# A change of order and of sums in a fused attention and dense-layer kernel on one core

## The chip, the cores and the metric

The kernel runs on one core of a Trainium2 chip. The metric is the device time of one execution in microseconds. "Before" is the kernel that is changed, "after" is the changed one. TensorE multiplies matrices, ScalarE computes tanh and exp, VectorE and GpSimd do elementwise work, and the sync engine issues most of the DMAs; the trace calls it SPq.

## The reference, cut to what matters

```python
def _attn_ref(q, k, v, cap):                      # (8, 12, 448, 64), f32
    scores = np.matmul(q, k.transpose(0, 1, 3, 2)) / np.sqrt(64)
    scores = cap * np.tanh(scores / cap)          # cap = 30
    attn = np.exp(scores - np.max(scores, axis=-1, keepdims=True))
    attn = attn / (np.sum(attn, axis=-1, keepdims=True) + 1e-09)
    return np.matmul(attn, v)

x = attn_out.transpose(0, 2, 1, 3).reshape(3584, 768)
g = np.maximum(x @ w1, x @ w2)                    # 768 -> 1024
out = g @ w_out                                   # 1024 -> 768
```

## The kernel before

Heads are taken in pairs, 48 in all. Three pairs are a *group*, whose k, q and v are loaded, cast and transposed together, so there are 16 groups. Two pairs are a *quad*, so there are 24 quads. Iteration `t` of the main loop computes the scores of quad `t + 1`, and the product with v and the sums of exponentials of quad `t`. A token row has 448 = 3 x 128 + 64 keys; the last 64 are the *left tokens*.

The normalization goes a long way round. VectorE copies the sums, one DMA brings them into shape (`sums`), VectorE inverts them, a DMA writes 7 KB of reciprocals to DRAM (`rec_d`), two DMAs read them back spread over 128 partitions (`rec_b`, here called the broadcast), and GpSimd multiplies (`xT`). GpSimd also casts k, q and v. From group 4 on, a DMA transpose makes `qkT` of the casts. Each engine works through its own list in order, and so does the sync engine: an issue that waits holds up all issues behind it.

```python
def add(t, ab, step):                    # sums of exponentials on VectorE
    if t < NS or t >= NQ:                # NS = 5: quads 0 to 4 sum on TensorE alone
        return
    ...
    if step == 0:
        nc.vector.tensor_add(d, e_of(t, ab, 1 if ab else 0), e_of(t, ab, 2 if ab else 1))
    else:
        nc.vector.tensor_add(d, d, e_of(t, ab, 0 if ab else 2))

def pv(t, ab):
    ...                                  # product with v
    if ab:
        for m in range(2):               # left tokens: two 128*64 matmuls
            nc.tensor.matmul(ss[64 * m : 64 * m + 64, :S], ones2, expo[t, 2][:, m, :], start=True, stop=False)
        nj = NJ if t < NS else 1
        for j in range(nj):
            for m in range(4):
                x = e_of(t, m // 2, j)[:, m % 2, :] if t < NS else esum[t][:, m, :]
                nc.tensor.matmul(ss[32 * m : 32 * m + 32, :S], ones, x, start=False, stop=(j == nj - 1))
    if ab == 0:
        U[t] = upool.tile([P, 2, S], f32, name="u", bufs=3)
    ...                                  # copy to U; copy sums, DMA them into sums[t]

def invert(t):
    r = xpool.tile([32, 56], f32, name="rec_s")
    nc.vector.reciprocal(r, sums[t])
    recd[t] = dram.tile([32, 56], f32, name="rec_d")
    nc.sync.dma_start(out=recd[t], in_=r)

def spread(t):
    ...
    for h in range(2):                   # waits until rec_d has landed
        nc.sync.dma_start(out=rec[t][64 * h : 64 * h + 64, :, :], in_=lines[h : h + 1, :, :].to_broadcast([64, 2, S]))

for g in range(2, NL):                   # what an iteration loads and casts
    if g < NT:
        ...
    else:
        e = 3 * g - g % 2
        at(e - 8, load, g, "k")
        at(e - 8 + g % 2, load, g, "q")  # odd groups: q half an iteration after k
        at(e - 6, cast, nc.gpsimd, g, "k")
        at(e - 6, cast, nc.gpsimd, g, "q")
        at(e - 4, cross, g)              # the DMA transpose
        ...

for t in range(NQ):                      # main loop, cut to the order of things
    ...
    if t > 4:
        spread(t - 2)
    extra(i)                             # loads, casts, transposes of this half
    ...
    pv(t, 0)
    ...
    if t > 4:
        normalize(t - 2, 0)              # multiplies, behind the casts
        normalize(t - 2, 1)
    ...
    if t > 4:
        invert(t - 1)
    extra(i + 1)
    ...
    pv(t, 1)
    ...
```

## Time and profile before

| | before |
|---|---|
| median of 4 runs | 378.8 us (375.2 to 382.1) |
| span of the profiled run (one of 380.9 us, not of the four), granted TensorE clock | 379.2 us, 0.980 |
| fourth exp of quad 2, 7, 8, 23 ends | 44.7, 114.7, 126.5, 319.5 us |
| dense matmuls alone at the end | 59.7 us |

The windows and waits that carry the bound are in the prediction.

Columns are the start and duration in us, engine, line, operation and tiles. This is the kernel before, around 114.7 us, when iteration 7 begins:

```profile
107.62 0.33 SPq L365 DMA_DIRECT2D rec_d<-rec_s  x1
107.99 0.43 SPq L137 DMA_DIRECT2D qr<-in_q_dram  x1
...
111.07 0.60 SPq L357 DMA_DIRECT2D sums<-st  x1
111.78 1.21 SPq L435 DMA_DIRECT2D out_dram<-osb  x2
113.09 1.83 SPq L371 DMA_DIRECT2D rec_b<-rec_d  x2
115.02 4.41 SPq L268 DMA_TRANSPOSE qkT<-kqf  x1
```

The reciprocals are written at 107.62; a q load, the sums and two stores are issued before the broadcast at 113.09, which by then need not wait; the transpose starts at 115.02, 0.3 us into iteration 7. The issue of this transpose occupies the sync engine for 4.41 us.

### The profile page before, as it was taken

The page shows a single profiled execution, that of the slowest core. Times are in us where ns is not written, and L with a number is a line of the kernel's source. Part 1 is how long each engine was busy: PE and PEld are TensorE (multiplying, and loading weights), DVE is VectorE, ACT ScalarE, POOL GpSimd, SP SyncE. Part 2 cuts the span into 40 slices and gives each one's busy share as a digit, 9 for nine tenths or more (in the row PEclk, how much of TensorE's full clock was granted, in tenths as well). Part 3 has the DMA queues.
Part 4 walks back from the last instruction along what each step waited for, and adds up shares of the span by engine and source line. Part 5 has one row for each costly group of instructions (what it writes and reads, how often), then busy time and mean ns, then how long its engine had stood idle before and what let it go on. Part 6 is the DMA issues. An engine that isn't in the chain of part 4 may idle for free.

```text
span 379.2 us, 6549 instructions
## 1 busy us (share of the span) xinstructions
PE 349.0 (92%) x2492; PEld 168.2 (44%) x2492; DVE 200.6 (53%) x348; ACT 281.8 (74%) x265; POOL 150.1 (40%) x188
## 2 busy tenths in 40 slices
PE   3677986898999999999999999999989999999996
PEld 2223443443444444444444454434434444555563
DVE  4223473567665676455745654557448556633421
ACT  4999986697999989998898899889958897000000
POOL 3734135637554445444562456243644302420000
PEclk9997898999999999999999999999989999999999
DMA  7999999996788987999698959896988132422022
GB/s 251 263 209 220 274 284 223 227 193 139 215 212 221 213 232 203 223 234 255 177 213 208 251 163 250 232 242 165 216 217 213 51 91 105 122 80 95 2 83 84
DMA packets 104464, 71.56 MB, mean 189 GB/s; under 512 B 58224, under 2 KB 99440, under 8 KB 104432
## 3 DMA queue, kind: packets, MB, share of 16 engines
q1 hardware_dynamic: 102480, 67.99, 71.1%
q0 software_dynamic: 1952, 3.15, 4.5%
q8 instruction: 19, 0.31, 0.4%
q14 instruction: 13, 0.11, 0.1%
HBM read 53.48 MB, written 11.18 MB: 171 GB/s over the span
## 4 chain that ended last, share of the span: by engine, by line
PE 65%; DMA 19%; DVE 5%; SPq 4%; ACT 3%; issue 2%; POOL 1%; POOLq 0%; DVEq 0%; ACTq 0%
PE mm L396 17%; PE mm L411 16%; PE mm L408 12%; PE pv L334 6%; DMA qkT<-kqf 6%; PE s L295 6%; DMA qr<-in_q_dram 6%; DMA vr<-in_v_dram 4%; DMA rec_b<-rec_d 3%; PE pv L348 3%; PE ss L347 2%; PE s L290 1%; DVE u L351 1%; ACT expo L303 1%; ACT tanh L296 1%
## 5 line engine op out<-in xcount | busy, mean ns | idle before, releaser
L296 ACT ACTIVATE tanh<-s 128x896 bf16<-128x896 f32 x144 | 124.3, 915 | 32.5 <-PE s L295 31.1
L303 ACT ACTIVATE expo<-tanh 128x1792 bf16<-128x1792 bf16 (+1 forms) x96 | 144.9, 1510 | 0.1
L383 POOL TENSOR_TENSOR xT<-u,rec_b 128x448 bf16<-128x448 f32 x48 | 58.4, 1238 | 101.1 <-DMA rec_b<-rec_d 81.2
L411 PE MATMUL mm<-wo_sb,gT 128*128 128x384 bf16 x448 | 86.8, 330 | 0.0
L396 PE MATMUL mm<-xT,wd_sb 128*128 128x448 bf16 x384 | 79.1, 354 | 2.7 <-POOL xT L383 1.3
L351 DVE COPY u<-pv 128x448 f32<-128x448 f32 x48 | 29.9, 624 | 91.0 <-PE pv L348 78.3
L408 PE MATMUL mm<-wm_sb,xT 128*128 128x384 bf16 x336 | 66.6, 326 | 0.2 <-DVE gT L400 0.2
L411 PEld LDWEIGHTS <-gT 128*128 128x128 bf16 x448 | 43.6, 99 | 31.1 <-issue 3.6
L415 DVE COPY osb<-mm 128x384 f32<-128x384 f32 x56 | 31.1, 555 | 46.3 <-PE mm L411 46.0
L396 PEld LDWEIGHTS <-wd_sb 128*128 128x128 bf16 x384 | 37.2, 98 | 38.4 <-issue 5.9
L295 PE MATMUL s<-qkT 64*128 64x448 bf16 x288 | 43.2, 371 | 11.1 <-ACT tanh L298 3.4
L400 DVE TENSOR_SCALAR gT<-mm 128x448 bf16<-128x448 f32 x64 | 39.1, 616 | 16.8 <-PE mm L396 16.6
L408 PEld LDWEIGHTS <-xT 128*128 128x128 bf16 x336 | 32.5, 98 | 23.3 <-issue 1.9
L334 PE MATMUL pv<-expo,vp 128*64 128x448 bf16 x288 | 37.5, 370 | 0.0
L158 POOL CAST vp<-vr 128x1152 bf16<-128x1152 f32 x15 | 18.0, 1201 | 46.8 <-DMA vr<-in_v_dram 43.5
L321 DVE TENSOR_TENSOR esum<-esum,expo 128x896 bf16<-128x896 bf16 x38 | 29.9, 787 | 1.5
L319 DVE TENSOR_TENSOR esum<-expo 128x896 bf16<-128x896 bf16 x38 | 26.6, 699 | 0.0
L295 PEld LDWEIGHTS <-qkT 64*128 64x128 bf16 x288 | 9.4, 95 | 36.8 <-issue 28.7
L298 ACT ACTIVATE tanh<-s 128x896 bf16<-128x896 f32 x24 | 22.0, 917 | 4.4 <-PE s L290 3.9
L334 PEld LDWEIGHTS <-vp 128*64 128x64 bf16 x288 | 12.4, 110 | 21.3 <-issue 15.2
L232 PE MATMUL mm<-wo_sb,w2T 128*128 128x384 bf16 x96 | 19.1, 334 | 1.4 <-DVE qkT L264 1.4
L178 POOL CAST kqf<-qr 128x1152 bf16<-128x1152 f32 x12 | 14.5, 1207 | 9.6 <-DMA qr<-in_q_dram 9.4
(56 smaller groups left out, 227.7 us busy)
## 6 DMA issues: line engine op xcount, KB each, us to landing
rec_b<-rec_d SPq DMA_DIRECT2D x48, 224.0 KB
kr<-in_k_dram SPq DMA_DIRECT2D x12, 576.0 KB
qr<-in_q_dram SPq DMA_DIRECT2D x12, 576.0 KB
vr<-in_v_dram SPq DMA_DIRECT2D x12, 576.0 KB
out_dram<-osb SPq DMA_DIRECT2D x17, 384.0 KB
out_dram<-osb SPq DMA_DIRECT2D x22, 192.0 KB
osb<-in_moe_w_dram SPq DMA_DIRECT2D x6, 512.0 KB
vr<-in_v_dram SPq DMA_DIRECT2D x8, 288.0 KB
```

What stands on the lines that cost most here:

```text
L295: nc.tensor.matmul(s[:, h, :S], k0[r, j * P : (j + 1) * P], qTn[r, :])
L296: nc.scalar.activation(tanh[t, p][:, 2 * m : 2 * m + 2, :], s[:, :, :S], AF.Tanh, scale=scale / cap)
L303: nc.scalar.activation(expo[t, p], tanh[t, p][:, 0:n, :], AF.Exp, scale=float(cap))
L321: nc.vector.tensor_add(d, d, e_of(t, ab, 0 if ab else 2))
L334: nc.tensor.matmul(ps[r, :S], vp[g % 2][:, 2 * n + h, j, :], e_of(t, ab, j)[:, h, :], start=(j == 0), stop=False)
L351: nc.vector.tensor_copy(U[t][:, ab, :], ps[:, :S])
L383: eng.tensor_mul(xT[b // 2][:, hp, cs], U[t][:, ab, :], rec[t][:, ab, :])
L396: nc.tensor.matmul(ps[:, :S], wd_sb[:, c, f * P : (f + 1) * P], x[:, c, cs], start=(c == 0), stop=(c == KC - 1))
L400: nc.vector.tensor_relu(g[:, f, cs], ps[:, :S])
L408: nc.tensor.matmul(ps[:, : DM // 2], x[:, c, ts], wm_sb[:, c, hs], start=(c == 0), stop=False)
L411: nc.tensor.matmul(ps[:, : DM // 2], g[:, f, ts], wo_sb[:, f, hs], start=False, stop=(f == FC - 1))
L415: nc.vector.tensor_copy(osb[:, hs], ps[:, : DM // 2])
```

## The change

The intent was to take away the waits of the early quads and some of TensorE's work. Early v rows are loaded in one piece of 1792 bytes and cut up by the casts; `u` gets a fourth buffer; early loads are placed one by one; q of every group is loaded with its k; the broadcast is issued half an iteration sooner; multiplies stand ahead of casts; the exp of the left tokens is added on VectorE instead of by two matmuls; only quads 0 and 1 still sum on TensorE alone. The diff, cut to its core:

```diff
-        if step == 0:
+        if step == 2:                          # left tokens
+            r = slice(64 * ab, 64 * ab + 64)
+            d = esum[t][r, ab::2, :]
+            nc.vector.tensor_add(d, d, expo[t, 2][r, :, :])
+        elif step == 0:
...
-            for m in range(2):
+            for m in range(2 if t < NS else 0):
...
-            U[t] = upool.tile([P, 2, S], f32, name="u", bufs=3)
+            U[t] = upool.tile([P, 2, S], f32, name="u", bufs=4)
...
-    NS = 5
+    NS = 2
...
-            at(e - 8 + g % 2, load, g, "q")
+        at(e - 8, load, g, "q")
...                                             # early loads in a table of their own
-        if t > 4:
-            spread(t - 2)
+        if t > 3:
+            normalize(t - 2, 0)
+            normalize(t - 2, 1)
         extra(i)
...
         pv(t, 0)
-        F(8 + more8)
+        F(4)
+        add(t, 1, 0)
+        F(3 + 2 * more8)
...
-        if t > 4:
-            normalize(t - 2, 0)
-            normalize(t - 2, 1)
...
+        add(t, 0, 2)
         F(2 + more8 if more else 0)
-        add(t, 1, 0)
-        F(4 if more else 2)
+        add(t, 1, 2)
+        F(4 + more8 if more else 2)
         add(t, 1, 1)
...
+        if t > 2:
+            spread(t - 1)
         pv(t, 1)
```

More of the change, by code (lines that the diff above doesn't have):

```diff
@@ L118, in load @@
         t, m, l = raw_of(g, what)
-        if g < NT and what == "v":
-            x = rows(src, b, h0, h1).rearrange("(h r) c -> r h c", r=64)
-            for a in range(2):
-                nc.sync.dma_start(
-                    out=m[64 * a : 64 * a + 64, 2 * n0 : 2 * n1, :], in_=x[:, :, NJ * D * a : NJ * D * (a + 1)]
-                )
-            for par in range(2):
-                nc.sync.dma_start(
-                    out=l[64 * par : 64 * par + 64, n0:n1, :], in_=x[:, par::2, 2 * NJ * D :]
-                )
-            return
         if g < NT:
@@ L156, in cast @@
         x, m, l = raw_of(g, what)
+        if what == "v" and g < NT:
+            x = x[:, : L * S].rearrange("p (n c) -> p n c", c=S)
+            for h in range(2):
+                r = slice(64 * h, 64 * h + 64)
+                for a in range(2):
+                    eng.tensor_copy(
+                        vp[g % 2][64 * a : 64 * a + 64, h::2, :, :].rearrange("p n j d -> p n (j d)"),
+                        x[r, :, NJ * D * a : NJ * D * (a + 1)],
+                    )
+                eng.tensor_copy(vl[g % 2][r, :, r], x[r, :, 2 * NJ * D :])
+            return
         if what == "v":
@@ L346, in pv @@
                     x = e_of(t, m // 2, j)[:, m % 2, :] if t < NS else esum[t][:, m, :]
-                    nc.tensor.matmul(ss[32 * m : 32 * m + 32, :S], ones, x, start=False, stop=(j == nj - 1))
+                    nc.tensor.matmul(ss[32 * m : 32 * m + 32, :S], ones, x, start=(t >= NS), stop=(j == nj - 1))
         nc.tensor.matmul(ps[:, :S], vl[g % 2][:, n, :], expo[t, 2][:, ab, :], start=False, stop=True)
         if ab == 0:
-            U[t] = upool.tile([P, 2, S], f32, name="u", bufs=3)
+            U[t] = upool.tile([P, 2, S], f32, name="u", bufs=4)
         nc.vector.tensor_copy(U[t][:, ab, :], ps[:, :S])
@@ L453, in at @@
         todo[i].append((f, a))
-    for g in range(2, NL):
-        if g < NT:
-            e = 0 if g == 2 else 1
-            at(3 * g - 6 + e, load, g, "k")
-            at(3 * g - 6 + e, load, g, "q")
-            at(3 * g - 4 + e, load, g, "v")
-            at(3 * g - 4, cast, nc.gpsimd, g, "k")
-            at(3 * g - 4, cast, nc.gpsimd, g, "q")
-            at(3 * g - 2, cast, nc.gpsimd, g, "v")
-        else:
-            e = 3 * g - g % 2
-            at(e - 8, load, g, "k")
-            at(e - 8 + g % 2, load, g, "q")
-            at(e - 6, cast, nc.gpsimd, g, "k")
-            at(e - 6, cast, nc.gpsimd, g, "q")
-            at(e - 4, cross, g)
-            at(e - 4, load, g, "v")
-            at(e - 2, cast, nc.gpsimd, g, "v")
-    at(1, load, 1, "v")
-    at(2, cast, nc.gpsimd, 1, "v")
-    for c, i in enumerate((3, 3, 4, 5, 6, 7)):
-        todo[i].insert(c if i == 3 else 0, (load_w1, (c,)))
-    MS = 3
+    for g in range(NT, NL):
+        e = 3 * g - g % 2
+        at(e - 4, cross, g)
+        at(e - 8, load, g, "k")
+        at(e - 8, load, g, "q")
+        at(e - 4, load, g, "v")
+        at(e - 6, cast, nc.gpsimd, g, "k")
+        at(e - 6, cast, nc.gpsimd, g, "q")
+        at(e - 2, cast, nc.gpsimd, g, "v")
+    early = {
+        1: [(load, (1, "v"))],
+        2: [(load, (3, "k")), (load, (3, "q")), (load_w1, (0,))],
+        3: [(load_w1, (1,)), (load_w1, (2,)), (load, (2, "v"))],
+        4: [(load_w1, (3,))],
+        5: [(load_w1, (4,)), (load, (3, "v"))],
+        6: [(load_w1, (5,))],
+    }
+    for i, what in ((2, "2k"), (2, "2q"), (2, "1v"), (4, "2v"), (5, "3k"), (5, "3q"), (6, "3v")):
+        early[i].append((cast, (nc.gpsimd, int(what[0]), what[1])))
+    for i, x in early.items():
+        todo[i] += x
+    MS = 2
     fill_const(nc.vector, 0)
@@ L486 @@
     load(0, "v")
+    load(2, "k")
+    load(2, "q")
     cast(nc.vector, 0, "k", 0, 1)
@@ L489 @@
     fill_const(nc.gpsimd, 1)
+    load_w2(0)
+    load_w2(1)
     transposes(0)
@@ L502 @@
     transposes(2)
-    cast(nc.vector, 0, "v")
     cast(nc.gpsimd, 1, "k")
@@ L507 @@
         load_wo(f)
-    for c in range(3):
-        load_w2(c)
-    for c in range(3, KC):
+    for c in range(2, KC):
         load_w2(c)
@@ L527 @@
         weights(i)
-        if t % 3 == 2 and t > 2:
+        if t % 3 == 2 and t > 5:
             fill_q.append(moe(t // 3 - 1))
@@ L537 @@
             transposes(i + 3)
-        F(5 + more8 if more else 0)
-        if t > 4:
-            spread(t - 2)
+        if t == 0:
+            cast(nc.vector, 0, "v")
+        F(4 + more8 if more else 0)
+        if t > 3:
+            normalize(t - 2, 0)
+            normalize(t - 2, 1)
         extra(i)
-        F(6 if more else 3)
+        F(5 + 2 * more8 if more else 3)
         if more:
@@ L546 @@
         pv(t, 0)
-        F(8 + more8)
+        F(4)
+        add(t, 1, 0)
+        F(3 + 2 * more8)
         F(3 if more else 0)
-        if MS < i <= MS + KC:
-            subtract(i - MS - 1)
-        if t > 4:
-            normalize(t - 2, 0)
-            normalize(t - 2, 1)
+        if 3 <= i < 3 + KC:
+            subtract(i - 3)
         if more:
@@ L557 @@
         weights(i + 1)
+        if t == 4:
+            fill_q.append(moe(0))
         if i + 4 < NT * L:
             transposes(i + 4)
+        add(t, 0, 2)
         F(2 + more8 if more else 0)
-        add(t, 1, 0)
-        F(4 if more else 2)
+        add(t, 1, 2)
+        F(4 + more8 if more else 2)
         add(t, 1, 1)
         F(2 if more else 0)
-        if t > 4:
+        if 1 < t < 4:
+            spread(t - 2)
+        if t > 2:
             invert(t - 1)
-        elif t > 1:
-            spread(t - 2)
         extra(i + 1)
-        F(3 + more8 if more else 0)
+        F(2 + more8 if more else 0)
         if more:
@@ L573 @@
             ex(t + 1, 2)
+        if t > 2:
+            spread(t - 1)
         pv(t, 1)
@@ L578 @@
         F(3 if more else 0)
-        if 0 < t < 5:
+        if 0 < t < 3:
             invert(t - 1)
-        if 1 < t < 5:
+        if 1 < t < 4:
             normalize(t - 2, 0)
             normalize(t - 2, 1)
-        if MS < i + 1 <= MS + KC:
-            subtract(i - MS)
-    F(6)
-    spread(NQ - 2)
-    F(10)
+        if 3 <= i + 1 < 3 + KC:
+            subtract(i - 2)
+    F(16)
     invert(NQ - 1)
```

## The prediction

> **What bounds the kernel now.** The 48 pairs of heads run as 24 quads of two. A quad needs four rounds of tanh and exp on ScalarE; between them TensorE does scores, the product with v, sums of the exponentials, and "fills", matmuls of the dense layer put into gaps. I first read the whole page (TensorE 92%, ScalarE 74%, VectorE 53%), then the timeline of ScalarE for the end of each quad's fourth exp (21.1, 44.7, 88.1, 102.9, 126.5 us after quads 0, 2, 5, 6, 8; the last exp at 319.5), and asked for the windows between these times:
>
> ```profile
> core 0: us, PE busy (x) PEld busy (x) DVE busy (x) ACT busy (x) POOL busy (x), PEclk, DMA share, GB/s
> 21.10:44.70 23.60, 18.48 (x213) 8.04 (x209) 7.82 (x13) 23.37 (x22) 7.71 (x12) 0.86 1.07 224
> 44.70:88.10 43.40, 35.88 (x358) 18.07 (x357) 25.57 (x39) 35.02 (x33) 20.14 (x24) 0.96 0.94 225
> 88.10:102.90 14.80, 14.09 (x88) 5.93 (x87) 10.35 (x18) 11.73 (x12) 8.40 (x13) 1.00 0.90 226
> 102.90:126.50 23.60, 23.60 (x161) 11.20 (x161) 12.87 (x23) 23.36 (x22) 12.06 (x14) 1.00 0.79 201
> 126.50:319.50 193.00, 189.52 (x1219) 88.18 (x1219) 113.70 (x193) 173.64 (x164) 83.94 (x97) 0.99 0.80 198
> 319.50:379.20 59.70, 55.96 (x333) 31.42 (x329) 22.77 (x40) 0.00 (x0) 6.68 (x6) 0.99 0.26 84
> ```
>
> Read the quads per window. Two quads in 23.60 us with ScalarE 99% busy: 11.8 us is the floor of a quad. The next three took 43.4 us instead of 35.4, the one after 14.8 instead of 11.8: 11.0 us lost while ScalarE waited. From 126.5 us TensorE is full and ScalarE 90% busy: 173.64/11.7 = 14.8 quads in 193 us, 13.0 us each, bound by TensorE. The last 59.7 us are dense matmuls alone. The waits from 44.7 to 103 us say who held ScalarE up:
>
> ```profile
> POOL xT L383 <- DMA rec_b<-rec_d: 18.9, 4, 7.6
> ...
> ACT tanh L296 <- PE s L295: 10.9, 8, 4.3
> ...
> DVE u L351 <- POOL xT L383: 5.6, 1, 5.6
> ...
> PE mm L262 <- DVE wm_sb L237: 5.1, 2, 3.7
> ```
>
> Read upward: GpSimd's multiply waits for the broadcast reciprocals; VectorE's copy of the next product waits for the multiply to free one of three `u` buffers (5.6 us); TensorE's transposes wait for a bank that VectorE, working in order, has not emptied (3.7 us); tanh waits 4.3 us at 68 us.
>
> **What the Trainium skill says.** "Perfetto Trace Analysis" (its opening note on roofline) calls matmul busy time a bad metric, since matmuls are pipelined. The trace agrees: a 448-column fill is recorded as 354 ns, but in the chain 48 take 9.08 us, 189 ns each; a 384-column one takes 162 ns (8 in 1.30 us). I count with these. "TensorEngine Tiling (Array Packing)", Key Properties: changing the tiling mode drains the array. The two 128*64 sum matmuls start 0.28 us before the next group (81.97 to 82.25), not 0.19, which fits. "SBUF — State Buffer", Who interferes with whom: a VectorE instruction with two SBUF inputs contends with a GpSimd instruction that reads SBUF, and the later one blocks. The adds of exponentials agree, between 615 ns and twice that:
>
> ```profile
> L319 DVE TENSOR_TENSOR esum<-expo x38: 615/616/1246, 84.4 to 320.7; 128x896 bf16<-128x896 bf16 x38
> L321 DVE TENSOR_TENSOR esum<-esum,expo x38: 615/625/1550, 87.1 to 322.0; 128x896 bf16<-128x896 bf16 x38
> ```
>
> "DMA: Bandwidth & Descriptors", Specifications: under 512 B a transfer misses line rate. In the DMA packets of the first 70 us a 256-byte packet took 24 ns, one of 768 bytes 53, one of 1792 bytes 98: 10.7, 14.5 and 18.3 bytes/ns.
>
> **The change part by part.**
>
> Rows of v, groups 0 to 3. Before, a group is 768 packets of 768 and 384 of 256 bytes: (768 x 53 + 384 x 24)/16 = 3.1 us of all DMA engines; after, 384 x 98/16 = 2.35 us. Four groups save 3 us of a DMA system that is 94 to 107% busy from 21 to 88 us, and 12 issues. In exchange a cast becomes four of 64x576 and two small ones: on GpSimd some 1.7 us more for each of three groups (estimated from 557 ns at 448 elements and 1201 at 1152), hidden by its idle time. On VectorE, v of group 0 is now cast after a transpose copy, some 2.5 us that may hold tanh up by 0.4 us.
>
> Placing. Group 3's k and q are loaded an iteration earlier, reciprocals are spread about half a quad sooner, multiplies stand ahead of casts, `u` has four buffers. All four act on the chain shown: the multiply of quad 0 finished at 63.3 us, and with a fourth buffer it is not needed until the ideal 80 us. The 4.3 us wait should vanish, and most of the small ones, since fills per quad before quad 8 fall from 44 to 40 (0.65 us).
>
> Sums, quads 2 to 4. Fourteen sum matmuls become four: by the timeline 0.97 us become 0.3, TensorE gains 0.65 us a quad. VectorE gets six adds a quad. Its load in iteration 2: two qkT copies 1.3, three wm 1.65, two w2T 1.36, two u and one st 1.86, reciprocal 0.48, two subtractions 2.5, six adds at 0.7 4.2: 13.3 us, less 19 overlaps of 0.08 (starts 0.53 us apart for 0.61 us recorded) = 11.8. VectorE is exactly full there, and in iteration 3.
>
> Sums, quads 5 to 23. The two 128*64 matmuls go: 0.28 us x 19, of which the 16 quads from 8 on are bound by TensorE: -4.5 us. VectorE gets two adds of 64x896, 1.3 to 2 us a quad. From 126.5 to 319.5 us it is 59% busy and would be about 70%; but in a quad with 448-column fills it is busy 9.6 of 13.1 us and would be near 11. A fill bank fills in 6 x 0.189 = 1.1 us and is emptied in 0.6; two adds in between can stall it. I take 1.5 us back.
>
> M sooner. By counting the yields the dense layer begins at the end of iteration 4, not in 5, but at 40 fills a quad both versions finish batch 0 at quad 8, and from there both spend 48. After the last scores 334 fills are left, before 329: +5 x 0.162 = +0.8 us.
>
> Sum, from 379.5 us: early waits -7 of the 11.0 (chosen: the buffer wait and half of the rest; VectorE full in two quads keeps the others); TensorE sums -4.5; VectorE stalls +1.5; the late wait at 264 to 281 us, where the chain shows a q load and a DMA transpose of 5.1 and 8.1 us, partly cured by loading q with k: -1; tail +0.8; start +0.4. Total -9.8: **369.7 us**.
>
> **Rivals.** *VectorE becomes the bound* in quads 2 to 5 and in the 448-column quads: for it, the sums above and adds that double beside GpSimd; against it, 53% busy overall and waits of 0.7 us in all of fills on VectorE's relu. Then the early gain is 3 us and the steady one 1: about 376. *The early DMA stays the wait*: its share is about 1, the bytes are nearly the same, and the two w2 loads now come before k and q of group 1 are in (2.8 us of DMA); the reciprocal broadcasts queue behind loads as before. Against: quads 1 and 2 ran at the floor with the DMA just as full, and every cast has an iteration of slack. It would leave 373 to 376. *Everything works*: all 11 us and all 4.5, quads from 8 on at 12.7 us, and the late stall gone: 363 to 365. *The loads are hidden anyway*: the wider rows alone are worth nothing; I believe that, the gain being in the order.
>
> **Range and chances.** The cases run from 363.5 to 376. Runs of the kernel before scatter from 375.2 to 382.1. Faster by over 2% means under 372: 67%. Within 2%: 31%. Slower: 2%, as only a new early stall could do it.
>
> **What would show it.** Right: quads 3 to 6 at 11.8 to 12.8 us each, the end of quad 8's exp near 119 us; no VectorE wait for xT; quads from 8 on at 12.7 to 12.9; two sum matmuls fewer per quad; adds of 64x896 near 0.6 us alone; a tail of about 60 us. Wrong: VectorE over 90% busy in 45 to 90 us with TensorE waiting for it; xT still waiting for the broadcasts; or quads from 8 on still at 13 us, which means that the matmuls removed turned into waits for VectorE.

## More of the kernel before

The profile's page of the kernel before gives the busy time of each engine with its share of the span, the busy tenths of GpSimd in 40 equal slices, and the chain of work that ended last, by engine:

```profile
PE 349.0 (92%) x2492; PEld 168.2 (44%) x2492; DVE 200.6 (53%) x348; ACT 281.8 (74%) x265; POOL 150.1 (40%) x188
...
POOL 3734135637554445444562456243644302420000
...
PE 65%; DMA 19%; DVE 5%; SPq 4%; ACT 3%; issue 2%; POOL 1%; POOLq 0%; DVEq 0%; ACTq 0%
```

TensorE is nearly full, and two thirds of the last chain are TensorE's own work. GpSimd is at 40% and under 80% in every slice: its work is spread evenly.

## The result, and the profile after

| | before | after |
|---|---|---|
| median of 4 runs | 378.8 us | 413.1 us (411.4 to 416.2) |
| profiled run: span, granted clock | 379.2 us, 0.980 | 414.4 us, 0.966 |
| quads 0 to 2 end at | 44.7 us | 46.3 us |
| quads 3 to 7 take | 70.0 us | 72.5 us |
| quads 8 to 23 take | 204.8 us | 230.6 us |
| dense matmuls alone | 59.7 us | 65.0 us |

A run is called slow when it takes over 1.5% more than the fastest of the same kernel. The four runs of the changed kernel were fast; of the kernel before, the one of 382.1 us is over that line and is left out of the ratio. The changed kernel is slower: the ratio is 1.095, with a 95% interval of 1.083 to 1.107. A ratio here is the mean time of one kernel's fast runs over the mean time of the other's fast runs of the same rounds, so it is not quite the ratio of the medians quoted. Ratios below are all to the kernel before, run on the same chip between the others.

The page of the kernel after, the same lines:

```profile
PE 354.2 (85%) x2424; PEld 167.7 (40%) x2424; DVE 252.5 (61%) x407; ACT 281.7 (68%) x265; POOL 169.6 (41%) x197
...
POOL 4940557455086407740481429330864420330000
...
PE 40%; DMA 22%; DVE 13%; SPq 7%; ACT 7%; POOL 5%; issue 4%; POOLq 0%; DVEq 0%; ACTq 0%
```

TensorE does no more work but has fallen to 85%. VectorE has 52 us more. GpSimd has slices near 0 beside slices of 6 to 9: it stands, and then catches up. The last chain now runs through DMA, VectorE and the sync engine instead of TensorE.

The windows of the kernel after, in the columns of the prediction: quads 3 to 5, quads 8 to 11, quads 12 to 23, and the end:

```profile
46.30:94.40 48.10, 37.54 (x334) 17.24 (x332) 37.49 (x56) 35.02 (x33) 28.21 (x31) 0.93 0.71 173
...
118.80:177.10 58.30, 49.79 (x301) 22.85 (x300) 36.60 (x57) 46.72 (x45) 31.63 (x34) 0.95 0.78 190
177.10:349.40 172.30, 154.65 (x958) 70.57 (x957) 113.68 (x179) 138.54 (x131) 72.10 (x78) 0.97 0.69 175
349.40:414.40 65.00, 58.62 (x334) 32.52 (x332) 26.08 (x43) 0.00 (x1) 7.39 (x6) 0.97 0.22 73
```

From 118.8 us TensorE, full before, idles 26 of 231 us, and the loss is not even: quads 8, 11, 14, 17 and 20 take 14.3, 16.1, 16.9, 16.5 and 18.6 us, while quads 10, 13, 16, 18 and 19 take 12.3 to 12.8. Every third quad is long, and mostly the one behind it: by the program these are the iterations in which an even group is transposed, for use in the next one. An odd group starts with the second pair of a quad, whose first scores are in the second of four rounds; that it escapes by this later need is argued from the program, not tested.

The waits of the kernel after from 118.8 to 349.4 us (total us, times, longest):

```profile
POOL xT L388 <- DMA rec_b<-rec_d: 100.1, 12, 15.5
ACT tanh L296 <- PE s L295: 40.7, 32, 4.3
...
DVE rec_s L368 <- DMA sums<-st: 19.3, 6, 5.7
...
PE s L295 <- DMA qkT<-kqf: 16.4, 5, 4.0
...
PE mm L413 <- DVE osb L420: 6.0, 3, 3.0
```

and those of the kernel before in the same stage, 114.7 to 319.5 us:

```profile
POOL xT L383 <- DMA rec_b<-rec_d: 42.3, 12, 4.6
...
ACT tanh L296 <- PE s L295: 14.7, 23, 2.3
...
PE s L295 <- DMA qkT<-kqf: 2.3, 2, 1.9
```

ScalarE's wait for scores grew by 26.0 us, the whole loss of these quads (25.8). TensorE idles 26.2 us here, 3.5 before. Most of this is in two kinds of wait: the scores wait 16.4 us for a DMA transpose (2.3 before), and the dense matmuls wait 9.1 us for VectorE to empty a bank (6.0 for `osb`, shown, and 3.1 for `gT`; 0.9 before). GpSimd's wait for the broadcast more than doubled, to as much as 15.5 us at a time, and VectorE waits 19.3 us for the sums (0.4 before).

One of the long quads, in the kernel after. First the sync engine, where iteration 7 begins at 118.8 us:

```profile
113.81 0.66 SPq L370 DMA_DIRECT2D rec_d<-rec_s  x1
119.08 1.23 SPq L376 DMA_DIRECT2D rec_b<-rec_d  x2
120.40 0.58 SPq L362 DMA_DIRECT2D sums<-st  x1
121.08 2.15 SPq L440 DMA_DIRECT2D out_dram<-osb  x2
123.43 3.94 SPq L268 DMA_TRANSPOSE qkT<-kqf  x1
```

then GpSimd (in brackets the idle time before and what ended it):

```profile
113.63 2.96 POOL L388 TENSOR_TENSOR xT<-u,rec_b 128x448 bf16<-128x448 f32 x2 [12.55 <-DVE rec_s L368]
...
118.83 1.15 POOL L178 CAST kqf<-kr 128x1152 bf16<-128x1152 f32 x1
...
122.62 0.78 POOL L183 CAST kqf<-qr 64x384 bf16<-64x384 f32 x1
```

and TensorE:

```profile
129.29 0.55 PE L295 MATMUL s<-qkT 64*128 64x448 bf16 x4 [3.35 <-DMA qkT<-kqf]
```

The broadcast now stands right behind the write that it reads, so the sync engine stands from 114.5 to 119.08 until that write has landed, and sums, stores and transpose come after. GpSimd stands 12.55 us ahead of a multiply, and the casts that the transpose needs stand behind it until 123.40. (The trace names a reciprocal of VectorE as what came last, ended at 113.59. The program has no such dependence: that reciprocal belongs to a later quad. The multiply needs a broadcast issued at 108.66, and the sums issued right behind that were in at 113.10, so I read it as a wait for the broadcast, like the 125.3 us that the list of the whole kernel names so.) So the transpose begins 4.6 us into its iteration instead of 0.3, and the scores of quad 9 wait 3.35 us for it.

The same trace shows this for all five even groups from here to iteration 19: the transpose begins 4.6 to 9.0 us into its iteration (0.3 to 2.2 before), within 0.1 us of the end of GpSimd's last cast and 0.1 to 1.6 us after the sync engine has finished the issue ahead of it. Two late paths end there almost together, so freeing one of them alone cannot free the transpose by much.

### The profile page after: what moved, and what is told of

It reads as the page before. It is cut to its first block, busy times and chain, and to the rows that moved or that the text cites. A ratio compares the mean times of both kernels' runs of the same rounds, so it can differ in the third digit from the quotient of the medians.

```text
span 414.4 us, 6453 instructions
## 1 busy us (share of the span) xinstructions
PE 354.2 (85%) x2424; PEld 167.7 (40%) x2424; DVE 252.5 (61%) x407; ACT 281.7 (68%) x265; POOL 169.6 (41%) x197
## 4 chain that ended last, share of the span: by engine, by line
PE 40%; DMA 22%; DVE 13%; SPq 7%; ACT 7%; POOL 5%; issue 4%; POOLq 0%; DVEq 0%; ACTq 0%
PE mm L401 11%; PE mm L416 9%; DMA rec_b<-rec_d 8%; PE mm L413 7%; DMA rec_d<-rec_s 7%; DMA qkT<-kqf 4%; PE s L295 4%; PE pv L339 4%; ACT expo L303 3%; ACT tanh L296 3%; DVE esum L322 2%; POOL xT L388 2%; DVE esum L324 2%; SPq L136 2%; PE mm L232 2%
## 5 line engine op out<-in xcount | busy, mean ns | idle before, releaser
L388 POOL TENSOR_TENSOR xT<-u,rec_b 128x448 bf16<-128x448 f32 x48 | 59.6, 1262 | 171.4 <-DMA rec_b<-rec_d 125.3
L416 PE MATMUL mm<-wo_sb,gT 128*128 128x384 bf16 x448 | 91.4, 342 | 0.0
L413 PE MATMUL mm<-wm_sb,xT 128*128 128x384 bf16 x336 | 70.4, 338 | 6.0 <-DVE osb L420 6.0
L295 PE MATMUL s<-qkT 64*128 64x448 bf16 x288 | 44.5, 380 | 24.0 <-DMA qkT<-kqf 16.4
L416 PEld LDWEIGHTS <-gT 128*128 128x128 bf16 x448 | 45.4, 102 | 33.8 <-issue 7.8
L405 DVE TENSOR_SCALAR gT<-mm 128x448 bf16<-128x448 f32 x64 | 39.6, 619 | 12.9 <-PE mm L401 12.6
L413 PEld LDWEIGHTS <-xT 128*128 128x128 bf16 x336 | 33.5, 101 | 31.8 <-issue 11.8
L326 DVE TENSOR_TENSOR esum<-esum,expo 128x896 bf16<-128x896 bf16 x44 | 37.0, 841 | 1.5
L322 DVE TENSOR_TENSOR esum<-esum,expo 64x896 bf16<-64x896 bf16 x44 | 35.9, 816 | 0.8
L324 DVE TENSOR_TENSOR esum<-expo 128x896 bf16<-128x896 bf16 x44 | 36.3, 824 | 0.0
L368 DVE RECIPROCAL rec_s<-sums 32x56 f32<-32x56 f32 x24 | 11.6, 485 | 21.1 <-DMA sums<-st 21.1
L339 PEld LDWEIGHTS <-vp 128*64 128x64 bf16 x288 | 12.5, 110 | 25.0 <-issue 16.3
```

The lines of the kernel that those rows point to most:

```text
L295: nc.tensor.matmul(s[:, h, :S], k0[r, j * P : (j + 1) * P], qTn[r, :])
L322: nc.vector.tensor_add(d, d, expo[t, 2][r, :, :])
L339: nc.tensor.matmul(ps[r, :S], vp[g % 2][:, 2 * n + h, j, :], e_of(t, ab, j)[:, h, :], start=(j == 0), stop=False)
L388: eng.tensor_mul(xT[b // 2][:, hp, cs], U[t][:, ab, :], rec[t][:, ab, :])
L405: nc.vector.tensor_relu(g[:, f, cs], ps[:, :S])
L413: nc.tensor.matmul(ps[:, : DM // 2], x[:, c, ts], wm_sb[:, c, hs], start=(c == 0), stop=False)
```

## The experiments

Medians are of 4 executions, of 6 in the last batch, slow ones included. Not all batches ran on the same chip. In the expectations letters stand for theories: **O**, the order of the chain (broadcast early, multiplies ahead of casts) holds up casts and transposes; **V**, the added VectorE work, with V2 for the sums of quads 2 to 4; **S**, VectorE, working in order, stands before the reciprocal until the sums are in; **Q**, q loaded with k delays the small DMAs behind it; **W**, the sync engine's own wait for the written reciprocals, ahead of the transposes; **C**, the casts behind the multiply as the whole of O's loss; **E**, the early part as a loss by itself.

### One order back: casts ahead of multiplies

```diff
# against after
+        extra(i)
         if t > 3:
             normalize(t - 2, 0)
             normalize(t - 2, 1)
-        extra(i)
```

> The changed kernel with one thing undone: in an iteration from quad 4 on, the casts, loads and DMA transposes come first and the multiply after them. Theory O (order): in the changed kernel GpSimd's in-order queue waits for the broadcast reciprocals in front of the casts of k and q, so every third iteration the DMA transpose is issued late and scores wait 3 to 6 us; then most of it comes back: below 395 us, quads after 7 at 13 to 13.5 us, TensorE's wait for qkT from the DMA transpose falls from 16.4 to under 5 us. Theory V (VectorE): the added adds of left tokens fill VectorE and block GpSimd; then nothing changes: 408 to 415 us.

Measured 406.2 us, ratio 1.074 (1.067 to 1.082), in between the two expectations. The wait of the scores for `qkT` fell from 16.4 to 8.2 us. So this order costs some 7 us and is one cause of several. With the casts out of the way, the five transposes still begin 2.8 to 8.3 us into their iterations, now right behind the sync engine's own late issues (within 0.05 us), 0.3 to 1.9 us after the last cast.

### Left tokens back on TensorE

```diff
# against after
         if step == 2:
+            return
-            for m in range(2 if t < NS else 0):
+            for m in range(2):
```

> The changed kernel with the left tokens summed on TensorE again (two more matmuls a quad) and the 44 adds of 64x896 gone from VectorE; all else as changed. Theory V: most comes back, below 392 us. Theory O: 405 to 415 us, qkT waits stay at 12 us or more, the long quads every third stay.

Measured 405.2 us, ratio 1.073 (1.065 to 1.082). Theory V wanted under 392 us; the scores still wait 12.1 us for `qkT`, as O had expected. The sums of left tokens, meant to gain 4.5 us, cost about 8 in this setting.

### The order of the chain alone, on the kernel before

```diff
# against before
-            spread(t - 2)
+            normalize(t - 2, 0)
+            normalize(t - 2, 1)
         extra(i)
...
+        if t > 4:
+            spread(t - 1)
         pv(t, 1)
```

> The kernel before, with only the places of the broadcast and the multiply from quad 5 on as in the changed kernel (broadcast at the end of an iteration, multiply ahead of the casts in the next). Theory O: 393 to 405 us, long quads every third, qkT waits over 12 us. Theory V: within 2% of 379 us.

Measured 395.9 us, ratio 1.050 (1.040 to 1.059). The long quads are back: quads 11, 14 and 20 take 15.7, 16.7 and 17.9 us, and the scores wait 10.5 us for `qkT` (over 12 had been expected). The reorder alone, with all VectorE work as before, does half of the damage.

### Left tokens alone, on the kernel before

The edit is that of the left tokens in the diff above.

> The kernel before, with only the left tokens of quads 5 to 23 summed by two adds of 64x896 on VectorE and the two 128*64 sum matmuls gone. Theory V: 390 us or more. Theory O: 374 to 383 us; by the prediction's own sum (4.5 us saved on TensorE, 1.5 us lost to stalls) 376 us.

Measured 383.1 and 381.7 us (fast), 389.8 and 388.1 (slow). Two fast runs give no interval; their mean is 1.2% above that of the fast runs before in the same batch. The groups of the adds in this kernel (busy us, mean ns):

```profile
L325 DVE TENSOR_TENSOR esum<-esum,expo 128x896 bf16<-128x896 bf16 x38 | 34.5, 907 | 1.8
L321 DVE TENSOR_TENSOR esum<-esum,expo 64x896 bf16<-64x896 bf16 x38 | 31.9, 839 | 1.2
```

and in the kernel before:

```profile
L321 DVE TENSOR_TENSOR esum<-esum,expo 128x896 bf16<-128x896 bf16 x38 | 29.9, 787 | 1.5
```

The new adds take 839 ns and the second of the old ones gets slower by 120 ns (by the groups, the first by 58). In the quads 9 to 23 VectorE is busy 146.0 us (113.7 before), and TensorE idles 7.7 us where it idled 3.5. Nearly all of the 7.7, 7.6 us, are waits for VectorE (0.9 before): 4.2 for adds that the sums need and 3.4 for full banks. The gain turned into waits for VectorE.

The gain itself was smaller than predicted. In the kernel before, the pair of `128*64` matmuls starts 0.186 us after the product's last matmul, and the four `128*32` sums start 0.286 us after the pair. In this kernel, in the quads where nothing is waited for, the four sums start 0.283 us after the product. The pair's 0.286 us holds the change of tiling mode, from `128*64` to `128*32` matmuls, and that change stays. So taking the pair out saves 0.19 us a quad, 3.0 us in 16 quads, and not 0.28.

### Sums before the broadcast

```diff
# against after
+        pv(t, 1)
         if t > 2:
             spread(t - 1)
-        pv(t, 1)
```

> The changed kernel with two neighbouring statements swapped: the product pv of the quad, which issues the DMA of its sums, now stands ahead of the broadcast of the quad before. Theory S (queue of DMA issues): in the changed kernel the sync engine, which issues in order, waits 5 us for the reciprocals' write to land before it may issue the broadcast, and the sums of the next quad stand behind that wait, so a quad cannot be shorter than write + broadcast issue + sums + reciprocal, some 11 us plus what else is queued; with the swap 390 us or less, and VectorE's wait for sums falls from 21 us to under 8. Theory C (casts behind the multiply): no more than 5 us gained, 406 us or more.

Measured 410.0 us, ratio 1.085 (1.079 to 1.091). VectorE's wait for the sums, 21.1 us in the whole kernel after, is gone from its list, and the time hardly moves. The scores wait 18.5 us for `qkT`. Theory S, which wanted 390 us or less, is refuted: that wait was real, but removing it did not shorten the path.

### The chain back to its old order, all else as after

```diff
# against after
-        if t > 3:
-            normalize(t - 2, 0)
+        if t > 4:
+            spread(t - 2)
         extra(i)
...                       # multiplies back behind pv(t, 0)
-        if t > 2:
-            spread(t - 1)
```

> The changed kernel with the places of broadcast and multiply from quad 5 on as in the kernel before; early loads and sums as changed. If the chain costs 15 us or more, as in the run of the kernel before with the chain alone (16.9 us), this takes 390 to 397 us. If the parts only slow each other down together, below 385 us.

Measured 398.9 us, ratio 1.057 (1.051 to 1.062), just above the 390 to 397 expected: the order is worth about 14 us of the 36.

### The same, and left tokens back too

The edits are those of the chain and of the left tokens above, together.

> As the last, and the left tokens summed on TensorE again. What stays changed is the early part (loads, casts, adds in quads 2 to 4, M sooner). Theory E (the early part costs 4 us by itself, as the end of quad 7's exp at 118.8 instead of 114.7 us says): 381 to 386 us. If the early part is neutral or gains: 372 to 380 us.

Measured 392.1 us with one slow run, ratio 1.037 (1.032 to 1.042), above both expectations. Another 7 us. A loss of 14 us remained that neither O nor the left tokens explain. The sync engine of this kernel shows what was left:

```profile
148.37 0.59 SPq L125 DMA_DIRECT2D kr<-in_k_dram  x1
...
150.31 0.60 SPq L125 DMA_DIRECT2D qr<-in_q_dram  x1
...
152.49 0.68 SPq L371 DMA_DIRECT2D rec_d<-rec_s  x1
...
157.42 1.30 SPq L377 DMA_DIRECT2D rec_b<-rec_d  x2
158.83 5.35 SPq L268 DMA_TRANSPOSE qkT<-kqf  x1
```

All 1.3 MB of a group's k and q stand ahead of the 7 KB of reciprocals, and the broadcast can be issued 4.9 us after the write. In the kernel before, the write of the same iteration is issued at 147.60 with q behind it at 148.24, and the broadcast follows at 150.93, after 3.3 us. That gave theory Q.

### The broadcast early, the multiplies where they were

```diff
# against before
-        if t > 4:
-            spread(t - 2)
         extra(i)
...
+        if t > 4:
+            spread(t - 1)
         pv(t, 1)
```

> The kernel before with only the broadcast moved from 30% of an iteration to the end of the one before, ahead of pv; the multiply stays after the casts. Theory S: 388 us or more, with VectorE waiting over 12 us for sums. Theory C: within 1% of 379 us, since the casts stay ahead of the multiply.

Measured 388.2 us, ratio 1.028 (1.023 to 1.032). The early broadcast alone costs 2.8% of the 5.0% that it costs together with the multiplies; theory C, which wanted it harmless, fails. VectorE's wait for sums came to 21.8 us, as S had expected; the runs with the sums first (above and below) show that this is not what costs the time. The waits of the sync engine, in this kernel

```profile
SPq L371 <- DMA rec_d<-rec_s: 50.6, 20, 5.0
```

in the kernel before

```profile
SPq L371 <- DMA rec_d<-rec_s: 31.4, 14, 4.4
```

and in the kernel after

```profile
SPq L376 <- DMA rec_d<-rec_s: 66.8, 22, 5.3
```

show the engine that issues most DMAs standing longer and more often.

### q with k alone, on the kernel before

```diff
# against before
-            at(e - 8 + g % 2, load, g, "q")
+            at(e - 8, load, g, "q")
```

> The kernel before with one token changed: q of the odd groups from 5 on is loaded together with its k, half an iteration sooner, as in the changed kernel. Theory Q: the 0.6 MB of q then lie ahead of the 7 KB of reciprocals in the DMA queue, the write lands some 5 us after its issue, the sync engine waits for it before the broadcast, and the DMA transpose behind it is late: 384 us or more, with the sync engine's wait for that write over 42 us (31 before). By the prediction (an earlier q helps, 1 us) and by the theory that loads are hidden: 376 to 381 us.

Measured 387.2 us, ratio 1.025 (1.018 to 1.032; three fast runs, one slow). One term of one line of the source costs about 9 us. The sync engine's wait came to 38.5 us, less than the 42 that I had expected and still more than 31.4; GpSimd's wait for the broadcast rose from 81.2 to 106.5 us. The scores' wait for `qkT` rose from 2.3 to 6.3 us. The cost agrees with theory Q; the size of its named wait was missed.

### Chain, left tokens and q back

This is the kernel after with the three edits undone; of the change there remain the early part (rows, fourth `u` buffer, placed loads) and VectorE sums for quads 2 to 4.

> The changed kernel with the chain and the sums of left tokens back as before, and now the late q load of odd groups too. Theory Q: it takes back half or more of the 14 us that were still missing, 380 to 386 us. If the missing 14 us are the early part or the spread of the fills: 389 us or more.

Measured 381.9 us, ratio 1.012 (1.004 to 1.021). The q load is worth another 9 us.

### Wide rows and the fourth buffer alone, on the kernel before

```diff
# against before
-        if g < NT and what == "v":
-            ...                        # four DMAs of 768- and 256-byte rows
+        if what == "v" and g < NT:     # in cast(): four large casts and two small ones
+            ...
-            U[t] = upool.tile([P, 2, S], f32, name="u", bufs=3)
+            U[t] = upool.tile([P, 2, S], f32, name="u", bufs=4)
```

> The kernel before with v of groups 0 to 3 in 1792-byte rows and the casts that go with them, and a fourth buffer for u; places unchanged. The wait of 5.6 us of VectorE for the multiply at 58 to 63 us should go with the fourth buffer. If the early stall is that buffer: 372 to 376 us, quad 4 under 14 us. If it is the DMA and VectorE behind it: 377 to 381 us.

Measured 374.6 us, ratio 0.992 (0.986 to 0.998). Quad 4 takes 13.2 us instead of 17.2. From 44.7 to 103 us the waits of this kernel have:

```profile
ACT tanh L296 <- PE s L295: 7.4, 10, 2.1
```

VectorE's wait of 5.6 us for a free `u`, shown in the prediction, is no longer in its list, and ScalarE waits 7.4 instead of 10.9 us.

### Sums before an early broadcast, on the kernel before

```diff
# against b_spread_early of the text above
+        pv(t, 1)
         if t > 4:
             spread(t - 1)
-        pv(t, 1)
```

> The kernel before with the broadcast moved to the end of the iteration before, but behind pv and its sums (the run with the broadcast ahead of pv took 388 us). Theory S, the sums behind the wait: 378 to 382 us, VectorE's wait for sums under 6 us. If instead what matters is that the sync engine waits at all, ahead of the loads and transposes: 385 us or more.

Measured 390.3 us with one slow run, ratio 1.030 (1.021 to 1.039): not better than 388.2, though VectorE's wait for sums fell to 2.8 us. Theory S is refuted a second time. The sync engine's wait for the write fell too, from 50.6 to 39.6 us, and the scores' wait for `qkT` rose from 4.4 to 8.4: the sum of the sync engine's waits does not by itself set the time.

### The early broadcast issued by GpSimd

```diff
# in spread(), on top of the early broadcast
-            nc.sync.dma_start(
+            nc.gpsimd.dma_start(
```

> The kernel before with the early broadcast (388 us when the sync engine issues it), now issued by GpSimd, so that no wait for the reciprocals' write stands before the DMA transposes on the sync engine. Theory W (that wait delays the transposes): 382 us or less, TensorE's waits for qkT under 3 us. If the DMA queue's order or contention is the cause: 386 us or more, with qkT waits as they were (6.0 and 4.4 us).

Measured 382.6 us with one slow run, ratio 1.009 (0.995 to 1.023). The time speaks for theory W, but the interval reaches nearly to that of the early broadcast from the sync engine, and the chips differ. The profile does not help W. The transposes are issued early in it, 0.6 to 2.9 us before their iterations begin, and the scores still wait 6.1 us for them, which was the sign of the rival, order or contention in the DMA queue. This point stays open.

### VectorE sums for quads 2 to 4 alone

```diff
# against before
-    NS = 5
+    NS = 2
```

> The kernel before with one constant changed: from quad 2 on, not 5, the exponentials are added on VectorE (four adds of 128x896 a quad). The prediction: TensorE gains 0.56 us a quad, 1 to 2 us in all: 376 to 378 us. Theory V2 (VectorE, in order, is then late with the copies of transposes in quads 2 to 4): 380 us or more, with TensorE waiting over 5 us for VectorE's copies in the first 100 us.

Measured 382.8 us, ratio 1.013 (1.004 to 1.022), some 5 us, but its profile does not show 5 us where I looked for them: quad 8 ends at 127.2 us (126.5 before). Quads 14 and 15 take 14.9 and 15.2 us instead of 12.2 and 13.6, though the change touches nothing there. In this one profile the early delay is small, and later quads lose more: before quad 14 ends, the scores of quad 15 wait 2.6 us for a transpose, and why that is late was not found. Theory V2's sign did not appear: in the first 100 us TensorE waits 12.1 us for VectorE, 13.9 in the kernel before. The profiled run of the kernel before was one of 380.9 us, so this comparison of profiles can show only 2 of the 5 us.

### The left adds without their gain

The two adds of left tokens are made into a spare tile, and the matmuls stay.

```diff
# against before
+        if step == 2:
+            r = slice(64 * ab, 64 * ab + 64)
+            z = att.tile([P, 2, S], bf16, name="spare", bufs=1)
+            nc.vector.tensor_add(z[r, :, :], d_of(t)[r, ab::2, :], expo[t, 2][r, :, :])
```

> The kernel before with two adds of 64x896 a quad on VectorE as for the left tokens, but into a spare tile, and TensorE's sums kept: the cost of the adds without the gain. The adds replacing the matmuls took 385.6 us. If the matmuls are worth the predicted 0.28 us a quad: 388 to 392 us. If they are worth nothing where VectorE is waited for: 383 to 386 us. The adds being harmless would be 377 to 380 us.

Measured 388.8 us, ratio 1.028 (1.013 to 1.043). The adds alone cost about 10 us (5 to 16 by the interval). With the matmuls removed the loss was 1.2%. The difference puts the matmuls at a rough 1.5%, 6 us, but one of the two comparisons has no interval and the other is wide; the 3.0 us read from the trace above is the better figure.

### Rows and buffer with the broadcast issued by GpSimd

The edit is that of rows and buffer, with `nc.gpsimd.dma_start` in `spread()`.

> The kernel before with v in wide rows and four buffers for u (374.6 us), and the broadcast issued by GpSimd at its old place. If the sync engine's waits for the write (31 us in all before) hold transposes up even in the kernel before: 368 to 373 us. If they were hidden: 374 to 377 us, or worse by the two issues a quad that GpSimd now makes.

Measured 380.4 us, ratio 1.007 (0.995 to 1.020): no gain over the same kernel with the sync engine's broadcast at 374.6. In its place in the old order the broadcast is not worth moving to another engine.

### Only the early part of the change

The kernel after, with chain, left tokens and q back and `NS = 5`.

> The changed kernel with everything back as before but the early part. The prediction gave the early part 7 us: then 370 to 373 us. By subtraction (1.012 with the VectorE sums of quads 2 to 4, which alone cost 1.013) it is worth nothing: ratio 0.99 to 1.01.

Measured 374.6 us, ratio 0.992 (0.987 to 0.996), in five rounds. Quads 3, 5 and 6 take 11.9, 12.1 and 12.0 us as predicted; but quad 1 takes 13.3 instead of 11.8 and quad 4 still 16.3.

### Wide rows and the fourth buffer, again

> The kernel before with wide rows of v in groups 0 to 3 and four buffers for u, once more. If the gain is real: ratio 0.985 to 0.998. If it was scatter: 0.997 to 1.005.

Measured 375.8 us, ratio 0.994 (0.989 to 0.998), in five rounds beside the last one. Both beat the kernel before by under 1%, and cannot be told apart. They are the best versions found. The edit is that of the rows and buffer above, run again.

## Why the prediction was wrong

It said 369.7 us; the kernel took 413. Undoing the change step by step shows the terms. Each row has the edits of the rows above it too; the third column is the difference of the ratios, times 378 us. The ratios' intervals are 0.5 to 1.2% to either side, so a term is good to some 3 us:

| kernel | ratio to before | worth |
|---|---|---|
| after | 1.095 | |
| chain in its old order | 1.057 | 14 us |
| left tokens back on TensorE | 1.037 | 7 us |
| q of odd groups after k | 1.012 | 9 us |
| sums of quads 2 to 4 back on TensorE | 0.992 | 8 us |
| what is left: the early part | | -3 us |

Done one at a time on the kernel before, the chain costs 5.0%, q 2.5%, the left tokens 1.2%, the sums of quads 2 to 4 1.3%, and rows and buffer give 0.8% back. These add up to 9.2%, against 9.5% for all together. Within the intervals, the parts do not need each other to do harm.

**"Placing".** The prediction said that reciprocals spread sooner, multiplies ahead of casts, earlier loads and a fourth buffer "all four act on the chain shown". Two of them had the wrong sign. Spreading sooner moves the broadcast right behind the write it depends on, and puts the landing time of 7 KB into the sync engine's list, ahead of everything else it issues; multiplies ahead of casts put the same wait into GpSimd's list, ahead of the casts. Both end at the DMA transposes. The prediction weighed the broadcasts only where they hurt, in 45 to 103 us, and not what stood behind them in the two lists from 115 us on, where the chain was not on the path. One of its own signs of being wrong came true: the multiply still waits for the broadcasts, 125.3 us in all (81.2 before). The order that looked late, broadcast half an iteration after the write and multiplies behind casts, hid a latency. Shown: the early broadcast costs 2.8%, the whole reorder 5.0%, the order back gains 14 us. In the kernel with the early broadcast alone, the four transposes of even groups from iteration 10 on begin 2.1 to 4.8 us into their iterations (0.4 to 2.2 before), right behind the sync engine's issue ahead of them and 0.2 to 1.6 us after the last cast: there the sync engine holds them. Whether its wait for the write makes it late, or a fuller DMA queue, the GpSimd experiment could not settle.

**"Partly cured by loading q with k: -1".** The late wait at 264 to 281 us was read as a load that came late. Moving it costs 2.5%. The prediction asked when q arrives, and not what 0.7 MB more, ahead of a 7 KB write in the same queue, delays.

**"TensorE sums -4.5" and "VectorE stalls +1.5".** The first was mis-sized: the 0.28 us holds a change of tiling mode that stays when the pair goes, and the saving is 0.19 us a quad, 3.0 us. The second was mis-sized by far more: the adds alone cost about 10 us. The prediction had named the mechanism, two adds in front of the copy that empties a bank, and put 1.5 us on it; it left out that the adds make the other adds slower too (907 instead of 787 ns) and that TensorE's sums would then wait for them. The prediction's own wrong-sign test, quads from 8 on still at 13 us, points the right way, but it is too fine: its 13.0 us comes from a division of busy times, and counted by the ends of the exps, quads 9 to 23 took 12.9 us each before (193.0/15) and 13.1 with the left adds (196.0/15).

**"Early waits -7 of the 11.0".** The early part is worth 3 us. The buffer wait went as predicted, and with only the early part quads 3, 5 and 6 are at 12 us; quad 1 lost 1.5 us and quad 4 kept 4.5 of its 5.4 us of loss. "VectorE exactly full" for quads 2 to 4 was a warning in the prediction's own words: in the kernel after VectorE is busy 12.8 and 13.6 us in quads 3 and 4, over the 11.8 us floor that the prediction's sum had reached, and they take 14.9 and 17.5 us. So VectorE is over its floor there, but not busy throughout, and it is not the whole of that loss. I called that a rival that ends at 376 us. By the ladder these sums cost 8 us, alone 5; where the profile loses them was not found.

**"Tail +0.8".** It grew by 5.3 us. At its head the multiply, moved there, lies beside the last adds (the timeline of VectorE after):

```profile
351.52 2.09 DVE L322 TENSOR_TENSOR esum<-esum,expo 64x896 bf16<-64x896 bf16 x2
353.65 1.44 DVE L326 TENSOR_TENSOR esum<-esum,expo 128x896 bf16<-128x896 bf16 x1
```

Three adds take 3.5 us, and TensorE's last sums wait 2.5 us for them. With the left tokens back the tail is 62.8 us, with the chain back 61.7, with both 60.2.

**What was right.** Wide rows alone were taken as worth little; no run had them alone. With rows and the fourth buffer VectorE's wait for a free `u` is gone, as predicted. VectorE as a bound was named as a rival, and TensorE's waits for it did grow. "Slower: 2%, as only a new early stall could do it" was wrong in its reason as well: the stall was not early.

**What stays open.** How the 14 us of the chain divide between the sync engine's standing, GpSimd's late casts and fuller DMA queues; where the cost of the VectorE sums for quads 2 to 4 falls; and what the earlier start of the dense layer and the other placings of fills did by themselves, which no run took apart.

## What to carry to other kernels

A chain of small DMAs was cheap here as long as other issues lay between a write and the DMA that reads it back. Before moving a DMA or a multiply forward, list what stands behind it in its engine's queue and which of that has no slack. A bulk load put ahead of a small write that something waits for cost 2.5% here. When work is taken from one engine, read the saving from the starts on that engine with and without it: the change of tiling mode stayed here. Test moves of order one at a time: of all the parts here, only the wide rows and the fourth buffer, run together, and the early part that holds them were worth keeping, for 0.6 to 0.8%.

## What the Trainium skill lacked or had wrong

- "DMA: Bandwidth & Descriptors", Two DMAs through the same engine are not ordered: it says to make the issuing engine wait for the first DMA's semaphore before it issues the dependent one. It lacks what this wait costs everything behind it in that engine's list: here 22 waits, 66.8 us, up to 5.3 us each, for writes of 7 KB.
- The same page, Issuing engines are not separate DMA queues: initiating a DMA is "usually small relative to the DMA itself". A DMA transpose needs an exception: here the issue of one held the sync engine for 3.9 to 5.4 us in the lines shown, of 5.9 us between the start of the issue and the first scores that used it (123.43 to 129.29).
- "SBUF — State Buffer", Who interferes with whom: the rule that an add of two SBUF inputs contends with a GpSimd instruction that reads SBUF agrees with the runs. It gives no size for a mix: in the kernel after, adds at which GpSimd is idle take 0.62 us on average; all together average 0.82 to 0.84 us, and reach 1.6 us.
- "TensorEngine Tiling (Array Packing)", Key Properties, gives no size for the drain at a change of tiling mode. Here a matmul starts 0.19 us after one of 448 columns in the same mode, and 0.28 to 0.30 us after it when the mode changes (product to sums, sums to product, fills to scores): about 0.1 us a change.
